# Issuing the first K load and the load of q ahead of the start-up barrier in a single-query attention kernel

## The chip, the cores and the metric

The kernel runs on one core of a Trainium2 chip. The metric is the device time of one execution in microseconds (us). The kernel before takes 321.4 us. The span that a profile shows runs from the first to the last instruction that it recorded; it is about 1.5 us shorter than the time. A load is issued by one instruction; its data then run as packets (16 KB each in a 2 MB load) on 16 DMA engines, and it has landed when all 16 have told so.

## The reference

One query row per head attends to 8192 keys, for 16 heads of 256 elements, all in bf16:

```python
B, H, Sq, Sk, D = 1, 16, 1, 8192, 256
scores = jnp.einsum("bhqd,bhkd->bhqk", q, k) * D ** -0.5
p = softmax(scores, axis=-1)
return jnp.einsum("bhqk,bhkd->bhqd", p, v)
```

K and V are 67.1 MB each and every element is used once, so the work is mostly reading 134.2 MB.

## The kernel before

SyncE (SP) issues every load of K and V; each head's K and V lie in one of two buffers. VectorE (DVE) computes most scores as products of K with a q that is spread over the partitions (`prod`), TensorE (PE) transposes a quarter of the K columns and scores those, and later multiplies the probabilities with V (`acc`). ScalarE (ACT) loads q and evacuates PSUM. GpSimd (POOL) writes constants.

A recording layer collects the operations of each engine with the names that they wait for. Operations that wait for nothing may be emitted ahead of the block of the engines' programs, in front of everything else (the comments in this excerpt are added):

```python
    def emit_front(self, e, eng, n):
        for i in range(n):
            assert not self.ops[e][i][2]        # waits for nothing
            self.run(e, eng, i)
        self.front[e] = n
# ... cut ...
        plan.op("act", lambda e: e.dma_start(q16[:, :], q[0, :, 0, :]), "q", dma=(s_q, 16))
# ... cut: one plan.op("sp", ... dma_start ...) for each piece of K and V, in order ...
        plan.resolve(sems, alias)

        plan.emit_front("sp", nc.sync, K_SLOTS)     # four K loads: heads 0 and 1, two halves each
        plan.emit_front("act", nc.scalar, 1)        # q

        with nc.Block() as block:
            # ... cut: each engine emits the rest of its program
```

What the source does not show: when the program object `nc` is made, the assembler puts four memsets of its own constants on POOL, and behind them a barrier of all five engines. On each engine that is a drain, which tells POOL that the engine has come, and a wait for POOL's release. This kernel reads none of those constants: no instruction in its trace has one of them as input. Its first instruction of its own still stands behind the barrier.

## Time and profile before

| kernel before | us |
|---|---|
| time, median of 3 runs at first | 321.43 |
| span of the profiled run | 319.86 |
| release of the barrier, as SP sees it | 0.64 |
| first K load: issue, first packet, landed | 0.72, 1.73, 8.64 |
| q: issue, landed | 0.72, 4.32 |
| first DVE product | 8.82 |
| last V piece landed | 317.49 |

The page of the kernel before gives the DMA activity in 40 slices of the span (tenths busy, then GB/s), and the groups of instructions by cost (out<-in, shapes, count, busy us, mean ns, idle before and what ended most of it):

```profile
DMA  7999999999999999999999999999999999999995
GB/s 301 434 436 429 422 426 426 424 426 428 427 426 428 434 445 430 438 414 447 414 451 434 418 447 410 451 434 422 438 414 447 414 429 432 428 426 417 422 412 198
...
HBM read 134.23 MB, written 0.01 MB: 420 GB/s over the span
...
L374 DVE CUSTOM_DVE_ANT_0 prod<-Kb,qbc 128x256 bf16<-128x256 bf16 x768 | 268.5, 410 | 26.0 <-DMA Kb<-in_k_dram 23.5
...
Kb<-in_k_dram SPq DMA_DIRECT2D x18, 2048.0 KB, 19.3
```

Only the first and the last slice are not full of DMA, and between them the rate stays at 410 to 451 GB/s in every slice. The last line says that a 2 MB K load lands 19.3 us (median) after its issue, though 2 MB take 4.9 us at this rate: in the middle of the stream several loads are in the queue. DVE is busy for 86% of the span, but most of its idle time ends when a K load lands. So the kernel is a stream of loads, with a start before it and a tail behind it. (The page's chain of waits gives DVE 52% of the span and DMA 41%, since DVE's last product on a K buffer frees it for a later load.)

The table by stage says the same (start:end and length in us, the engines' busy us and instruction counts, then PE's granted clock, the DMA share and the rate):

```profile
0.00:1.73 1.73, 0.00 (x0) 0.00 (x0) 0.00 (x0) 0.56 (x1) 1.07 (x7) 1.00 0.00 0
1.73:8.64 6.91, 1.34 (x6) 0.46 (x6) 0.00 (x0) 1.87 (x6) 0.81 (x6) 1.00 1.01 389
8.64:100.00 91.36, 60.09 (x577) 43.51 (x577) 89.75 (x519) 31.64 (x59) 0.00 (x0) 0.91 1.01 428
100.00:200.00 100.00, 72.14 (x720) 52.69 (x718) 91.22 (x528) 30.81 (x63) 0.00 (x0) 0.77 1.00 431
200.00:300.00 100.00, 76.22 (x716) 54.90 (x717) 92.57 (x535) 27.09 (x52) 0.00 (x0) 0.77 1.00 429
```

The Trainium skill, "DMA: Bandwidth & Descriptors", section "Where 436 GB/s comes from", puts the ceiling of a core's DMA fabric at 435 GB/s. The 427 to 431 GB/s of this trace are 98 to 99% of that. The stream itself can hardly be made faster; in the first 1.73 us it moves nothing at all.

The start, in the timeline of the kernel before (start and length in us, engine, line, operation; in brackets the idle time before and what ended it; a q behind an engine's name means its sequencer, which issues DMAs):

```profile
0.24 0.10 POOL L755 MEMSET const-float32-0.0<- 128x1 f32 x1 [0.24 <-issue]
...
0.72 0.41 ACTq L307 DMA_DIRECT2D q<-in_q_dram  x1
...
0.72 1.96 SPq L325 DMA_DIRECT2D Kb<-in_k_dram  x4
...
1.27 0.54 POOL L298 TENSOR_SCALAR identb<-off 128x128 bf16<-128x128 f32 x1
...
4.36 0.39 PE L427 MATMUL tp<-q,ones_rowb 1*128 1x256 bf16 x1 [4.36 <-DMA q<-in_q_dram]
...
8.82 0.42 DVE L374 CUSTOM_DVE_ANT_0 prod<-Kb,qbc 128x256 bf16<-128x256 bf16 x1 [8.82 <-DMA Kb<-in_k_dram]
```

And the first and last pieces of the chain of waits that ended last (start, length, what):

```profile
0.72 7.92 DMA Kb<-in_k_dram
...
303.09 13.14 DMA Vb<-in_v_dram
316.27 1.92 PE acc L617 x16
318.22 0.47 DVE o L632
```

The chain starts with the first K load and not with q: q is spread over the partitions by about 5.2 us, and DVE waits for K until 8.8 us. It ends with the last V pieces, the products on them, the scaling, and the store.

The timeline leaves out drains and semaphore instructions. The records of the trace have them (start and length in us, engine, operation):

```
0.000 0.007  SP    DRAIN            tells POOL
0.124 0.010  DVE   DRAIN            tells POOL
0.133 0.008  ACT   DRAIN            tells POOL
0.304 0.171  POOL  DRAIN            behind its four memsets
0.317 0.008  PE    DRAIN            tells POOL
0.519 0.017  POOL  EVENT_SEMAPHORE  all have come
0.597 0.017  POOL  EVENT_SEMAPHORE  release
0.639 0.017  SP    EVENT_SEMAPHORE  SP goes on
0.724 0.376  SP    DMA_DIRECT2D     first K load
```

SP comes to the barrier first and then waits for the others, the constants and the release.

### The profile page before, as it was taken

The numbers are of one execution on the slowest core, as the hardware profiler recorded it, in microseconds if no ns is written. First come the engines' busy times: TensorE is split into PE (matmuls) and PEld (weight loads), VectorE is DVE, ScalarE is ACT, GpSimd is POOL, SyncE is SP. The second block draws the span as 40 slices with busy tenths as digits, with TensorE's granted clock in tenths as the row PEclk, the third lists the DMA queues.
The fourth block names the chain that finished last, engine by engine and source line by source line (L and its number), as shares of the span: only waits on it lengthen the run. The fifth ranks groups of instructions, "written<-read, shape, count | busy, mean of one in ns | idle before, by whom it ended". The sixth has DMA issues, their size and how long they took to land.

```text
span 319.9 us, 6414 instructions
## 1 busy us (share of the span) xinstructions
PE 227.3 (71%) x2166; PEld 164.0 (51%) x2166; DVE 275.1 (86%) x1587; ACT 93.5 (29%) x184; POOL 1.9 (1%) x12
## 2 busy tenths in 40 slices
PE   1745238779596958679485794966669578868997
PEld 0514126556465735456354563654547446545774
DVE  0899999999999999897997979979798999999600
ACT  3453223331506042330603315042330514233010
POOL 2000000000000000000000000000000000000000
PEclk9999999959669875957879597695958859795899
DMA  7999999999999999999999999999999999999995
GB/s 301 434 436 429 422 426 426 424 426 428 427 426 428 434 445 430 438 414 447 414 451 434 418 447 410 451 434 422 438 414 447 414 429 432 428 426 417 422 412 198
DMA packets 8398, 134.36 MB, mean 420 GB/s; under 512 B 946, under 2 KB 963, under 8 KB 1860
## 3 DMA queue, kind: packets, MB, share of 16 engines
q1 hardware_dynamic: 8352, 134.22, 98.6%
q8 instruction: 5, 0.08, 0.1%
q14 instruction: 5, 0.04, 0.0%
q10 hardware_dynamic: 36, 0.02, 0.0%
HBM read 134.23 MB, written 0.01 MB: 420 GB/s over the span
## 4 chain that ended last, share of the span: by engine, by line
DVE 52%; DMA 41%; PE 4%; issue 2%; SPq 0%; DVEq 0%
DVE prod L374 49%; DMA Kb<-in_k_dram 29%; DMA Vb<-in_v_dram 12%; PE acc L617 4%; DVE S L374 2%; DVE g L347 1%; SPq L325 0%; DVE recip L356 0%; DVE o L632 0%; DVE m L393 0%; DVEq L158 0%; DVEq L155 0%; DVEq L152 0%
## 5 line engine op out<-in xcount | busy, mean ns | idle before, releaser
L374 DVE CUSTOM_DVE_ANT_0 prod<-Kb,qbc 128x256 bf16<-128x256 bf16 x768 | 268.5, 410 | 26.0 <-DMA Kb<-in_k_dram 23.5
L617 PE MATMUL acc<-Vb,E 128*1 128x256 bf16 x1024 | 142.9, 310 | 10.3 <-DMA Vb<-in_v_dram 10.1
L617 PEld LDWEIGHTS acc<-Vb,E 128*1 128x1 bf16 x1024 | 95.8, 95 | 53.4 <-issue 10.3
L513 ACT ACTIVATE KT<-tp 128x1024 bf16<-128x1024 bf16 x64 | 62.0, 1021 | 42.4 <-PE tp L504 42.4
L374 DVE DVE_READ_ACCUMULATOR2_ANT S<- 128x1 f32 x768 | 55.9, 73 | 0.0
L504 PE MATMUL tp<-identb,Kb 128*128 128x128 bf16 x512 | 46.4, 262 | 4.8 <-DMA Kb<-in_k_dram 4.7
L640 ACT ACTIVATE o<-acc,recip 1x256 bf16<-1x256 f32 x15 | 7.0, 465 | 134.6 <-PE acc L617 134.6
L504 PEld LDWEIGHTS tp<-identb,Kb 128*128 128x128 bf16 x512 | 39.5, 120 | 10.3 <-issue 7.4
L569 PE MATMUL misc<-g,ones_row 1*128 1x1 f32 x32 | 7.4, 297 | 34.8 <-DVE g L347 34.8
L530 PE MATMUL spe<-qcur,KT 128*128 128x1 bf16 x512 | 21.2, 166 | 15.3 <-ACT KT L513 15.3
L530 PEld LDWEIGHTS spe<-qcur,KT 128*128 128x128 bf16 x512 | 17.2, 103 | 21.1 <-ACT KT L513 20.9
L569 PEld LDWEIGHTS misc<-g,ones_row 1*128 1x128 f32 x32 | 6.0, 233 | 37.8 <-DVE g L347 37.6
L558 PE MATMUL misc<-ident,m 128*1 128x128 f32 x34 | 7.1, 294 | 16.3 <-DVE m L393 16.2
L558 PEld LDWEIGHTS misc<-ident,m 128*1 128x1 f32 x34 | 2.3, 83 | 18.7 <-DVE m L393 18.0
L576 ACT ACTIVATE negb<-misc 128x1 f32<-128x1 f32 x16 | 2.7, 172 | 25.7 <-PE misc L569 25.6
L347 DVE TENSOR_REDUCE g<-misc 1x1 f32<-1x128 f32 x17 | 4.7, 275 | 5.2 <-PE misc L558 5.2
L632 DVE TENSOR_SCALAR o<-acc,recip 1x256 bf16<-1x256 f32 x1 | 0.5, 471 | 8.2 <-PE acc L617 8.2
L598 PE MATMUL misc<-ones_col,lsum 128*1 128x1 f32 x34 | 3.2, 164 | 4.0 <-ACT E L583 3.6
L583 ACT ACTIVATE E<-S,negb 128x64 bf16<-128x64 f32 x16 | 5.6, 348 | 0.7 <-ACT negb L576 0.2
L356 DVE RECIPROCAL recip<-misc 1x1 f32<-1x1 f32 x17 | 2.6, 151 | 3.7 <-PE misc L598 3.7
L453 ACT ACTIVATE qbc<-qb 128x256 bf16<-128x256 bf16 x14 | 5.6, 400 | 0.0
L543 ACT ACTIVATE S<-spe 128x16 f32<-128x16 f32 x16 | 2.9, 184 | 7.5 <-PE spe L530 7.5
(26 smaller groups left out, 26.0 us busy)
## 6 DMA issues: line engine op xcount, KB each, us to landing
Kb<-in_k_dram SPq DMA_DIRECT2D x18, 2048.0 KB, 19.3
Vb<-in_v_dram SPq DMA_DIRECT2D x14, 2048.0 KB, 25.3
Kb<-in_k_dram SPq DMA_DIRECT2D x7, 4096.0 KB, 21.7
Vb<-in_v_dram SPq DMA_DIRECT2D x7, 4096.0 KB, 29.4
Vb<-in_v_dram SPq DMA_DIRECT2D x5, 1024.0 KB, 21.9
Vb<-in_v_dram SPq DMA_DIRECT2D x5, 512.0 KB, 12.4
Vb<-in_v_dram SPq DMA_DIRECT2D x2, 256.0 KB, 13.1
q<-in_q_dram ACTq DMA_DIRECT2D x1, 8.0 KB, 3.6
```

The lines of the kernel that those rows point to most:

```text
L347: lambda e: e.tensor_reduce(g[0:1, s : s + 1], misc[s][0:1, MT0 : MT0 + P], AX.X, ALU.max),
L374: lambda e, n=n, c=c, col=col, h=h, r=(ttr - 1) % PROD: e.tensor_tensor_reduce(out=prod[:, r * D : (r + 1) * D], in0=half(Kb, n, c * D, (c ...
L453: lambda e: e.activation(out=qbc[:, s * D : (s + 1) * D], in_=qb[:, (h - 2) * D : (h - 1) * D], func=ACT.Copy),
L504: lambda e, c=c, hf=hf, i=(b * NH + hf) * P, view=view: e.transpose(view[:, i : i + P], half(Kb, n, c * D + hf * P, c * D + (hf + 1) * P), ...
L513: lambda e, gn=gn, view=view: e.activation(out=KT[gn % KT_SLOTS][:, :], in_=view[:, 0 : GROUP * D], func=ACT.Copy),
L530: lambda e, b=b, hf=hf, oc=oc, gn=gn: e.matmul(spe[sl(h)][:, oc : oc + 1], lhsT=KT[gn % KT_SLOTS][:, (b * NH + hf) * P : (b * NH + hf + 1) ...
L558: lambda e: e.matmul(misc[s][0:1, MT0 : MT0 + P], lhsT=m[:, s : s + 1], rhs=ident[:, :], start=True, stop=True),
L569: lambda e: e.matmul(misc[s][:, BC0 : BC0 + 1], lhsT=ones_row[0:1, :], rhs=g[0:1, s : s + 1], start=True, stop=True),
L583: lambda e: e.activation(out=E[:, s * J : (s + 1) * J], in_=S[:, s * J : (s + 1) * J], func=ACT.Exp, bias=negb[:, h : h + 1], scale=SCALE, ...
L598: lambda e: e.matmul(misc[sl(h)][0:1, L0 : L0 + 1], lhsT=lsum[:, sl(h) : sl(h) + 1], rhs=ones_col[:, 0:1], start=True, stop=True,),
L617: lambda e, c=c, col=col: e.matmul(a[0:1, 0:D], lhsT=E[:, col : col + 1], rhs=half(Vb, n, c * D, (c + 1) * D), start=(x == 0 and c == 0), ...
L640: lambda e: e.activation(out=o[0:1, h * D : (h + 1) * D], in_=acc[s][0:1, 0:D], func=ACT.Copy, scale=recip[0:1, s : s + 1],),
```

## The change

The first K load and the load of q are emitted first, and a new function moves them in the instruction list in front of their engine's drain. The other three K loads stay behind the barrier. No instruction is added or removed on any engine; apart from line numbers, only the order on SP and ACT differs.

```diff
-        for i in range(n):
+        for i in range(self.front.get(e, 0), n):
             assert not self.ops[e][i][2]
             self.run(e, eng, i)
         self.front[e] = n
@@
+def ahead_of_barrier(nc, engines):
+    block = nc.cur_bb.bb
+    ins = list(block.instructions)
+    for eng in engines:
+        mine = [i for i in ins if i.engine == eng.engine]
+        last = max(n for n, i in enumerate(mine) if i.opcode == "EventSemaphore")
+        gate = ins.index(next(i for i in mine if i.opcode == "Drain"))
+        moved = mine[last + 1 :]
+        assert moved and all(i.opcode == "DMACopy" for i in moved), [i.opcode for i in moved]
+        ins = [i for i in ins if i not in moved]
+        ins[gate:gate] = moved
+    block.instructions = ins
@@
+        plan.emit_front("act", nc.scalar, 1)
+        plan.emit_front("sp", nc.sync, 1)
+        ahead_of_barrier(nc, (nc.sync, nc.scalar))
         plan.emit_front("sp", nc.sync, K_SLOTS)
-        plan.emit_front("act", nc.scalar, 1)
```

The intent is to start the stream while the barrier is still being gathered.

## The prediction

> **What bounds the kernel now.** A load stream. The page gives 134.23 MB of HBM reads at a mean of 420 GB/s; the stage table gives a DMA share of 1.00 to 1.01 and 427 to 431 GB/s from 8.64 to 300 us. DVE is busy 86%, but follows the loads (groups: 23.5 of its 26.0 us idle end with a K load). A middle load is issued some 20 us before it lands although 2 MB take 4.9 us of stream time, so the queue never runs dry. What is left is start-up and tail.
>
> Start-up, from the instructions in order of time: all engines meet at the barrier (drains at 0.00 to 0.32 us, POOL's constant memsets at 0.24 to 0.43 us, release at 0.64 us). SP issues the first K load at 0.72 us; its first packet runs at 1.73 us; it has landed at 8.64 us. ACT issues q at 0.72 us; it lands at 4.3 us. The first DVE product starts at 8.82 us, released by K, not by q. The chain of waits begins with this: 7.92 us of DMA from 0.72 us.
>
> **What the change does.** It adds and removes no instruction. One DMA issue on SP (0.38 us) and one on ACT (0.41 us) move ahead of their drains; the order listing shows that the second to fourth K load still wait for the release.
>
> - Gain: the first K issue moves from 0.72 to about 0.02 us, and its packets with it: 0.65 to 0.7 us.
> - Cost: SP reaches its drain at about 0.4 us and ACT at about 0.55 us. The last to arrive were PE (0.32 us) and POOL (0.48 us), so I estimate the release 0.1 to 0.2 us later, at 0.75 to 0.85 us. POOL's constants and DVE's loop set-up slip by that; they have over 3 us of slack: free.
> - The second K load is issued at about 0.9 instead of 1.16 us. The first keeps the stream busy until nearly 8 us, so no hole opens.
> - q: the Trainium skill, "DMA: Bandwidth & Descriptors", section "Issuing engines are not separate DMA queues", says that issuing from several engines saves only issue time; I expect nothing from q, which is not on the chain anyway.
>
> **How much is on the critical path.** All of the first load's shift: no idle stretch absorbs it, the buffer frees follow it, and the last V pieces, the last products (1.92 us), DVE's scaling and the store hang on the stream's end. Everything slides by about 0.65 us, a fifth of one per cent.
>
> **Predicted time:** 320.8 us, range 320.3 to 321.3. Chances: faster by over 2% 0.005, within 2% 0.985, slower by over 2% 0.01.
>
> **What would show it right.** The first K issue within 0.1 us of the span's start; its first packet at about 1.0 us, its landing at about 8.0 us; the release at 0.75 to 0.85 us; the second K issue before 1.0 us; later K landings about 0.65 us earlier; GB/s of the middle unchanged; span about 319.2 us. If the span itself starts later, compare times, not spans.
>
> **What would make it wrong.** (1) The 1.0 us from the first issue to its first packet may partly be set-up that ends at a fixed time; then little is gained. (2) A drain behind a DMA issue may wait for the whole transfer: then the second K load comes at about 8 us, a hole opens, and the kernel is slower by 1 us or more. (3) In the last loads some DMA engines end 1.8 us after the others; if instruction fetches move among them, several tenths may come or go. None reaches 2%.

## The result, and the profile after

The changed kernel takes 320.79 us (median of 6 runs, 320.74 to 321.0), the kernel before 321.46 us in the same rounds (321.33 to 321.64). The ratio is 0.998, with a 95% interval of 0.9967 to 0.9993. Ratios here are the mean time of one kernel's runs over that of the other's of the same rounds, so they are not quite the ratio of the medians. The gain of 0.67 us is real but a fifth of one per cent. A second set of five runs gave 320.72 us beside 321.48 us, ratio 0.9974 (0.9960 to 0.9987).

The start, in the timeline of the changed kernel:

```profile
0.00 2.49 SPq L341 DMA_DIRECT2D Kb<-in_k_dram  x4
0.12 0.38 ACTq L323 DMA_DIRECT2D q<-in_q_dram  x1
0.23 0.10 POOL L773 MEMSET const-float32-0.0<- 128x1 f32 x1 [0.23 <-issue]
...
1.46 0.54 POOL L314 TENSOR_SCALAR identb<-off 128x128 bf16<-128x128 f32 x1
...
4.28 0.39 PE L443 MATMUL tp<-q,ones_rowb 1*128 1x256 bf16 x1 [4.28 <-DMA q<-in_q_dram]
...
8.19 0.43 DVE L390 CUSTOM_DVE_ANT_0 prod<-Kb,qbc 128x256 bf16<-128x256 bf16 x1 [8.19 <-DMA Kb<-in_k_dram]
```

The origin of the clock has not moved: POOL's first memset stands at 0.23 us here and at 0.24 us before. So times can be read across. The K issue went from 0.72 to 0.00 us, and the first DVE product from 8.82 to 8.19 us. The identity came 0.19 us later. q's first use came only 0.08 us earlier, although q was issued 0.60 us earlier.

The records of the trace for the barrier:

```
0.000 0.366  SP    DMA_DIRECT2D     first K load
0.119 0.010  DVE   DRAIN            tells POOL
0.119 0.379  ACT   DMA_DIRECT2D     q
0.298 0.171  POOL  DRAIN            behind its four memsets
0.311 0.008  PE    DRAIN            tells POOL
0.419 0.126  SP    DRAIN            tells POOL
0.549 0.134  ACT   DRAIN            tells POOL
0.715 0.017  POOL  EVENT_SEMAPHORE  all have come
0.793 0.017  POOL  EVENT_SEMAPHORE  release
0.836 0.017  SP    EVENT_SEMAPHORE  SP goes on
0.921 0.327  SP    DMA_DIRECT2D     second K load
```

ACT is now the last to come, and the release is 0.20 us later. A drain behind a DMA issue took 0.13 us instead of 0.01 us; it did not wait for the transfer.

The rest of the profile is that of before, slid. The page, the table by stage, and the ends of the chain of waits of the changed kernel, cut as above:

```profile
DMA  9999999999999999999999999999999999999995
GB/s 353 427 429 426 427 427 427 423 427 423 426 429 427 431 446 448 423 435 419 444 415 448 439 419 439 419 444 415 444 444 419 419 426 429 429 427 424 418 410 196
```

```profile
0.00:1.73 1.73, 0.00 (x0) 0.00 (x0) 0.00 (x0) 0.82 (x1) 0.88 (x7) 1.00 0.64 142
...
100.00:200.00 100.00, 72.45 (x708) 52.43 (x708) 91.23 (x528) 30.20 (x60) 0.00 (x0) 0.77 1.01 433
200.00:300.00 100.00, 76.92 (x718) 55.08 (x717) 92.56 (x537) 27.08 (x52) 0.00 (x0) 0.77 1.00 428
```

```profile
0.00 8.02 DMA Kb<-in_k_dram
...
302.60 12.94 DMA Vb<-in_v_dram
315.58 1.92 PE acc L633 x16
317.53 0.47 DVE o L648
```

The first slice rises from 301 to 353 GB/s. Other slices differ by up to 36 GB/s, up or down, but the rates by stage stay. The last products start at 315.58 instead of 316.27 us, and DVE's scaling at 317.53 instead of 318.22 us: each 0.69 us earlier; the first DVE product is 0.63 us earlier and the first issue 0.72 us.

### The profile page after: what moved, and what is told of

It is laid out like the page before. It is cut to its first block, busy times and chain, and to the rows that moved or that the text cites. A ratio compares the mean times of both kernels' runs of the same rounds, so it can differ in the third digit from the quotient of the medians.

```text
span 319.2 us, 6414 instructions
## 1 busy us (share of the span) xinstructions
PE 228.5 (72%) x2166; PEld 164.0 (51%) x2166; DVE 275.1 (86%) x1587; ACT 93.5 (29%) x184; POOL 1.9 (1%) x12
## 4 chain that ended last, share of the span: by engine, by line
DVE 52%; DMA 41%; PE 4%; issue 2%; SPq 0%; DVEq 0%
DVE prod L390 49%; DMA Kb<-in_k_dram 29%; DMA Vb<-in_v_dram 12%; PE acc L633 4%; DVE S L390 2%; DVE g L363 1%; SPq L341 0%; DVE recip L372 0%; DVE o L648 0%; DVE m L409 0%; DVEq L158 0%; DVEq L155 0%; DVEq L152 0%
## 5 line engine op out<-in xcount | busy, mean ns | idle before, releaser
L633 PE MATMUL acc<-Vb,E 128*1 128x256 bf16 x1024 | 145.3, 314 | 11.1 <-DMA Vb<-in_v_dram 11.0
L633 PEld LDWEIGHTS acc<-Vb,E 128*1 128x1 bf16 x1024 | 96.9, 96 | 55.5 <-issue 11.0
## 6 DMA issues: line engine op xcount, KB each, us to landing
Vb<-in_v_dram SPq DMA_DIRECT2D x7, 4096.0 KB, 29.2
```

What stands on the lines that cost most here:

```text
L633: lambda e, c=c, col=col: e.matmul(a[0:1, 0:D], lhsT=E[:, col : col + 1], rhs=half(Vb, n, c * D, (c + 1) * D), start=(x == 0 and c == 0), ...
```

## The experiments

Three questions remain. Does the gain come from the K load alone (theory A: the time follows the issue of the first K load one for one, and nothing else of the change counts), or partly from q (rival B)? Does the later release cost something that a finer change would save (rival C)? And is the earlier issue of the other loads part of the gain (rival D), or does a stream with room hide part of any shift (rival E)?

Every kernel below computes the right result. This table has what their traces show; the time is the median of five runs (four for the last, nine for the kernel before in each of two sets of rounds), and the last column subtracts the median of the kernel before in the same rounds.

| kernel | first K issue | SP released | q landed | first K landed | last V landed | time | less before |
|---|---|---|---|---|---|---|---|
| before | 0.72 | 0.64 | 4.32 | 8.64 | 317.49 | 321.54, 321.48 | |
| changed (again) | 0.00 | 0.84 | 4.38 | 8.23 | 316.98 | 320.72 | -0.76 |
| K alone ahead | 0.00 | 0.70 | 6.18 | 7.95 | 316.77 | 320.82 | -0.72 |
| q alone ahead | 0.94 | 0.85 | 1.69 | 8.84 | 317.61 | 321.62 | +0.08 |
| four K and q ahead | 0.00 | 2.29 | 4.26 | 7.30 | 316.69 | 320.80 | -0.74 |
| first K later | 1.83 | 0.64 | 2.33 | 9.95 | 318.72 | 322.49 | +0.95 |
| second K at 5.1 us | 0.00 | 0.84 | 4.21 | 8.13 | 316.88 | 320.77 | -0.71 |
| second K at 10.4 us | 0.00 | 0.84 | 4.37 | 8.13 | 321.99 | 325.88 | +4.40 |

### The changed kernel again

It was run in the rounds of the last two experiments, unedited.

> The changed kernel itself, for comparison in the same rounds: 320.8 us, 0.7 us below the kernel before.

It was as expected: 320.72 us.

### K alone ahead of the barrier

```diff
-        plan.emit_front("act", nc.scalar, 1)
         plan.emit_front("sp", nc.sync, 1)
-        ahead_of_barrier(nc, (nc.sync, nc.scalar))
+        ahead_of_barrier(nc, (nc.sync,))
         plan.emit_front("sp", nc.sync, K_SLOTS)
+        plan.emit_front("act", nc.scalar, 1)
```

> Only the first K load is ahead of the barrier; q is issued after it again. Theory A (the time moves one for one with the issue of the first K load, nothing else counts): K is issued at about 0.0 us, release at about 0.72 us (SP's drain is the last but ends near 0.55 us), q lands at about 4.3 us, span about 319.2 us, time 0.65 us below the kernel before, the full gain. Theory B (a part comes from q's earlier issue): clearly less than 0.65 us, say 0.3 us.

The time is 320.82 us, 0.72 us below the kernel before (ratio 0.9978, 0.9964 to 0.9991): the full gain without q. One expectation was off. q did not land at 4.3 but at 6.18 us, 5.4 us after its issue. The timeline of this kernel:

```profile
0.78 0.39 ACTq L323 DMA_DIRECT2D q<-in_q_dram  x1
...
6.22 0.39 PE L443 MATMUL tp<-q,ones_rowb 1*128 1x256 bf16 x1 [6.22 <-DMA q<-in_q_dram]
...
8.13 0.42 DVE L390 CUSTOM_DVE_ANT_0 prod<-Kb,qbc 128x256 bf16<-128x256 bf16 x1 [8.13 <-DMA Kb<-in_k_dram]
```

DVE's first product still waits for K, so q's lateness cost nothing. But q now lands only 1.8 us before K, and its copy over the partitions comes between. q's move in the change buys margin, not time.

### q alone ahead of the barrier

```diff
         plan.emit_front("act", nc.scalar, 1)
-        plan.emit_front("sp", nc.sync, 1)
-        ahead_of_barrier(nc, (nc.sync, nc.scalar))
+        ahead_of_barrier(nc, (nc.scalar,))
         plan.emit_front("sp", nc.sync, K_SLOTS)
```

> Only the q load is ahead of the barrier. Theory A: no gain; since ACT comes later to the barrier (drain at about 0.55 us), the release comes at about 0.84 us and all four K loads are issued 0.2 us later (0.92 us): 0.2 us slower than the kernel before. Theory B (q matters): faster than before by 0.1 us or more. Side question: q landed at 4.2 to 4.3 us in both kernels whether issued at 0.12 or at 0.72 us; if it waits behind the first K packets, it lands here at about 2.5 to 3 us.

The time is 321.62 us, 0.08 us above the kernel before; the means differ by 0.13 us. This is no gain (ratio 1.0005, 0.9991 to 1.0018). The loss of 0.2 us that theory A asked for was not clearly seen: the first K issue came 0.21 us later, and a loss of 0.1 us can't be told from the scatter. q landed at 1.69 us, 2.6 us earlier than before, and DVE still started only with K. Rival B falls: q can land at 1.7 us or at 6.2 us without a trace in the time. The traces also show how long q waits when K is issued first. With no K load issued before it, its first packet ran 1.0 us after its issue; in the kernel before, with a K issue within 0.01 us of its own, 2.1 us after; with the first K issue 0.12 us ahead, as in the changed kernel, 2.8 us after; in the previous experiment, with it 0.78 us ahead, 4.0 us after. The K loads behind q do not set this: in the kernels with the first K issue 0.12 us ahead, the second K load came at 0.43, 0.92, 5.09 or 10.37 us, and q waited 2.7 to 2.8 us in all of them. Why the wait grows so is not shown.

### All four K loads and q ahead of the barrier

```diff
         plan.emit_front("act", nc.scalar, 1)
-        plan.emit_front("sp", nc.sync, 1)
-        ahead_of_barrier(nc, (nc.sync, nc.scalar))
         plan.emit_front("sp", nc.sync, K_SLOTS)
+        ahead_of_barrier(nc, (nc.sync, nc.scalar))
```

> All four K loads and q ahead of the barrier; SP's drain comes at about 1.8 us and the release at about 2.2 us, 1.4 us later than with one load moved. Theory A: the stream starts as in the changed kernel and is fed at all times, q and identity stay in time for the first K landing at 8.0 us: same as the changed kernel, 0.65 us below the kernel before. Theory C (a later release costs, because everything on POOL, PE, ACT and DVE starts later): 0.5 us to 1.4 us slower than the changed kernel, so no gain left or a loss against the kernel before.

SP was released at 2.29 us, 1.46 us later than in the changed kernel, and the time is 320.80 us (ratio 0.9977, 0.9963 to 0.9990): the same. Rival C falls: POOL, PE, ACT and DVE can start 1.5 us later at no cost. There is a second reading in this run. Its first K load landed at 7.30 us, 0.7 us earlier than in the changed kernel, and DVE started earlier with it:

```profile
7.49 0.43 DVE L390 CUSTOM_DVE_ANT_0 prod<-Kb,qbc 128x256 bf16<-128x256 bf16 x1 [7.49 <-DMA Kb<-in_k_dram]
```

DVE had 0.7 us more of a head start, and the kernel did not end earlier beyond the scatter. Since both effects lie in one run, a cost of the late release and a gain from the early DVE could cancel in the time. The trace speaks against that. The first of the 16 DMA engines was done with the first two loads at 6.98 and 11.87 us here, at 6.97 and 11.86 us in the changed kernel; and the fifth K load, the first that waits for a freed buffer, was issued 0.71 us earlier (16.08 us) but landed only 0.11 us earlier (38.28 us). The stream saw neither effect. (Why the first load landed earlier is told under "What sets the end of the stream".) So the useful effect is not that DVE begins earlier. It is that the stream does.

### The first K load later

The kernel before, where the first K load also waits for the identity matrix on POOL, and the other loads follow it in SP's order:

```diff
-                waits = []
+                waits = ["c_idb"] if (kind, h, i) == ("k", 0, 0) else []
@@
-        plan.emit_front("sp", nc.sync, K_SLOTS)
```

> The kernel before, with one thing added: the first K load also waits for the identity matrix on POOL (ready at 1.80 us), and the others follow it. Theory A: the issue moves from 0.72 to about 1.87 us, and the time rises by the same 1.15 us, to about 322.6 us. If some of the first microseconds were hidden by set-up that ends at a fixed time (the first packet not before some fixed moment), the rise would be smaller; if the later stream absorbs a late start, it would be near 0.

The chain of waits of this kernel now begins with POOL; its last pieces up to the load are:

```profile
1.26 0.54 POOL identb L298
1.81 0.02 issue
1.83 8.13 DMA Kb<-in_k_dram
```

The issue moved 1.10 us and the time rose by 0.95 us (ratio 1.0029, 1.0016 to 1.0043; I had expected 1.15 us for both); the landing of the last V piece moved 1.23 us in the one profile. With the changed kernel at 0.00 us this makes a line of three points: issue at 0.00, 0.72 and 1.83 us, times 320.8, 321.5 and 322.5 us. From end to end that is 1.7 us of time for 1.83 us of issue. The shift is not hidden by a set-up that ends at a fixed moment (the first packet ran 1.02, 1.01 and 1.02 us after these issues), and not absorbed later. I cannot tell a slope of 0.9 from one of 1.0 with a scatter of 0.1 us.

### The second K load later

The changed kernel, where the second K load and all behind it wait, in one kernel for the first copy of q (`qb0`), in the other for the first evacuated transpose (`ev0`):

```diff
-                waits = []
+                waits = ["qb0"] if (kind, h, i) == ("k", 0, 1) else []
@@
-        plan.emit_front("sp", nc.sync, K_SLOTS)
```

> The changed kernel, but the second K load (and all behind it) waits until the first copy of q is spread over the partitions, at about 4 to 5 us instead of 0.92 us. Theory A (only the stream's start counts, as long as its queue is fed before it runs dry): the first load's packets keep all engines busy until 7 us, the second load's first packets come about 1 us after its issue, at 5 to 6 us, so no hole opens: same as the changed kernel, 320.8 us. Rival D (the earlier issue of the other loads, 0.92 instead of 1.16 us, is part of the gain): 0.2 us or more slower, and with a delay of 4 us much more.

> The changed kernel, but the second K load waits for the first evacuated transpose, at about 10.2 us, when the first load has landed for 2 us. Theory A: a hole of about 3.6 us opens in the stream on the slowest DMA engine (its last packet ends near 7.6 us, the next can come near 11.2 us), and since nothing later has room to catch up, the time rises by the hole, 3 to 3.7 us, to about 324.2 us. Rival E (the stream has room and absorbs a late start; then the gain of the change would be something else): less than 1.5 us.

With `qb0` the second K load was issued at 5.09 us instead of 0.93 us, and the time is that of the changed kernel in the same rounds, 320.77 beside 320.72 us. Rival D falls: the loads behind the first one gain nothing by their earlier issue, as long as the first one's packets still run.

With `ev0` the issue came at 10.37 us. The page shows the hole in its second slice:

```profile
DMA  6699999999999999999999999999999999999995
GB/s 261 226 440 427 418 432 434 422 422 430 429 426 424 434 428 453 420 432 445 424 424 445 428 424 440 432 420 440 436 416 445 436 403 424 432 430 420 421 411 207
```

The time rose to 325.88 us, 5.2 us above the changed kernel (rival E falls: nothing is absorbed). The size that I had expected, 3 to 3.7 us, was too small, and the records say why. I had measured the hole on the slowest DMA engine, whose last packet of the first load ended at 7.69 us. The packets of the others ended at 6.6 to 7.05 us, and the next ones began at 11.32 to 11.92 us and took mostly 1.1 to 1.4 us each at first, where later packets took 0.61 us. On the mean of the 16 engines the last packet of the first load ended at 6.86 us and the next began at 11.53 us, a hole of 4.7 us; with 0.6 us of slow first packets that is 5.3 us. The engine that was slowest in the first load was the wrong one to measure: after the hole all 16 landed within 0.34 us of each other, and the 1.75 us by which the last engine trailed the first at the end of this run arose later, as the next part says.

### What sets the end of the stream

The trace has the time at which each of the 16 DMA engines tells that its share of a load has landed. Here they are for some loads of the changed kernel, sorted, in us behind the first of the 16:

```
landed at   engines in order of landing
  6.97      0.00 0.03 0.04 0.06 0.08 0.10 0.11 0.12 0.14 0.15 0.16 0.18 0.25 0.28 0.31 1.05
 26.54      0.00 0.02 0.03 0.04 0.04 0.06 0.09 0.09 0.11 0.12 0.13 0.14 0.25 0.28 0.29 1.07
 31.44      0.00 0.03 0.04 0.06 0.06 0.07 0.10 0.12 0.13 0.13 0.14 0.25 0.27 0.36 1.56 2.04
 90.09      0.00 0.06 0.08 0.09 0.12 0.13 0.14 0.18 0.23 0.33 0.77 1.59 1.64 1.86 1.90 2.11
314.75      0.00 0.05 0.11 0.16 0.16 0.20 0.21 0.22 0.32 0.90 1.44 1.55 1.58 1.81 1.86 2.05
```

The trace does not name the engines, but from one load to the next the pattern mostly stays within a few hundredths of a us, so an engine that has fallen behind stays behind, and the load has landed when the last engine is done. From time to time one engine falls further behind. Matching the 16 landings of one load with those of the next gives the sizes of these steps: 0.6 to 0.9 us or 1.5 to 1.7 us. Each time a packet of the queues that the page calls "instruction" ran during the load: one of 8 KB (0.31 us) at 6.10, 86.1, 260.1 and 306.8 us with the smaller steps, one of 16 KB (1.06 to 1.11 us) at 37.7, 60.6 and 77.1 us with the larger ones, and two, at 29.2 (16 KB) and 30.8 us (8 KB), ahead of the load that landed from 31.4 us on, where two engines fell behind. After those at 6.10, 60.6 and 260.1 us, the load packet that starts where they end can be told; it took 1.15, 1.11 and 0.99 us instead of 0.61. The last such packet, at 314.4 us, left the spread of the last load as it was. The Trainium skill, "Runtime: NRT & Kernel Launch", section "Instruction fetch mechanics", says that each engine refills its instruction memory in 16 KiB blocks over a DMA queue of its own; the 16 KB packets fit that, the 8 KB ones it does not explain, and the trace shows two such queues. At the end the last engine is 2.05 us behind the first (1.83 us in the kernel before). That these packets are the cause is read from their times; no run here took one away. One run moved one, beside other things: with four K loads ahead of the barrier the first 8 KB packet ran at 7.19 instead of 6.10 us, when the first load was nearly over. There all 16 engines were done with the first load within 0.33 us, and one was 0.91 us behind in the second load, where the changed kernel has one 1.05 us behind in the first. This is why the first K load of that run landed 0.7 us earlier. How much a better balance would give is open as well.

No run beats the changed kernel by more than the scatter. Four K loads ahead of the barrier, or K alone, are as good.

## Why the prediction was right

The prediction was 320.8 us and the measurement 320.79 us. Its steps, one by one:

- **The kernel is a stream of loads, and no idle stretch absorbs a shift.** Right. The stage rates stay at 427 to 433 GB/s, and the end moved by 0.69 us for 0.72 us at the start. A later first load and a hole after it both came through to the end, +0.95 us for 1.10 us and 5.2 us for a hole and slow first packets of 5.3 us together.
- **The first K issue moves from 0.72 to about 0.02 us, its packets with it.** Right: 0.00 us, and the first packet 1.02 us after the issue began, as before (1.01 us).
- **The barrier's release slips by 0.1 to 0.2 us and costs nothing.** Right: 0.20 us. A slip of 1.65 us against the kernel before was free too.
- **The second K issue moves to about 0.9 us; no hole opens.** Right: 0.92 us, and 5.09 us would have done.
- **Nothing from q.** Right: K alone gave the full gain, q alone none. The section of the skill that the prediction names here is not tested by this, since q was not on the chain.
- **What could have made it wrong.** The first packet is not held by a fixed moment. The drain took 0.13 us and did not wait for the transfer. In the tail, the spread of the engines grew from 1.83 to 2.05 us, so the earliest engine gained 0.92 us and the last one 0.69 us. This is the scatter that the third point named; it stayed at 0.2 us.

The time was hit more closely than it deserved: the gain was 0.67 us in the first rounds and 0.76 us in the second, so the prediction holds to about 0.1 us.

## What to carry to other kernels

When a kernel is one stream that never runs dry, time the first packet of that stream. In this kernel a wait in front of its first issue, at a barrier for constants that the kernel does not read, was paid about in full, and waits that only delayed other engines or later loads were free until the queue ran dry. Test both in another kernel with a dose: delay the first issue, then the second, and see which one the time follows. Before moving an instruction for speed, ask what its result waits for; q could land at 1.7 or 6.2 us without any effect, because K landed at 8.

## What the Trainium skill lacked or had wrong

- "DMA: Bandwidth & Descriptors", section "Latency and other measured facts", gives about 600 ns to the first byte for loads issued from SP and ACT. The runs agree only if one counts from the end of the issuing instruction: 0.65 us for the first K load of the changed kernel (end of issue 0.37 us, first packet 1.02 us), and 0.63 us for q issued alone. From the start of the issue it is 1.0 us. The page does not say from where it counts.
- The same page, section "Issuing engines are not separate DMA queues", says that loads issued from several engines interleave on the same DMA engines. I found no time on it that a small load then waits: q (8 KB, from ACT) had its first packet 1.0 us after its issue when no K load was issued before it, 2.1 us when one was issued with it, 2.7 to 2.8 us with one 0.12 us ahead, and 4.0 us with one 0.78 us ahead. In the last case it landed 5.4 us after its issue.
- No page that I found tells that a drain is slower behind a DMA issue: 0.13 us on SP and ACT, against 0.01 us without one.
- "DMA: Bandwidth & Descriptors" lacks that the first packets of a stream are slow: the first packet on a DMA engine took 0.9 to 1.5 us, later packets of the same 16 KB 0.61 us. After the hole at 7 to 11 us they were slow again, 1.2 us on the mean.
- "Runtime: NRT & Kernel Launch", section "Instruction fetch mechanics", calls the cost of crossing a 16 KiB boundary mostly hidden. It lacks that in an evenly split stream of loads each such packet seems to put one DMA engine behind for good: by 0.6 to 0.9 us after a packet of 8 KB and by 1.5 to 1.7 us after one of 16 KB, up to 2.05 us at the end of the changed kernel. The link is read from their times, and from one run in which such a packet came 1.1 us later and the step with it; no run took one away.
